# A kernel of attention, MLP and experts: an early unit's transposes moved by two iterations, row copies moved ahead of small steps, and a fold's first half in layer 1's bank

## The chip, the cores and the metric

One core of a Trainium2 chip runs the whole program. The metric is the device time of one execution in microseconds (us), as the median of several runs. Five engines work side by side, each through a queue of its own in order: TensorE (PE) does the matmuls, ScalarE (ACT) and VectorE (DVE) the elementwise work, GpSimd (POOL) small arithmetic and the indirect DMAs (gathers and scatters by a list of indices), SyncE (SP) issues the plain DMAs. They wait for each other only through semaphores.

## What is computed

Three stages, each feeding the next. (Cut from the reference.)

```python
# 1. attention with 32 memory slots per head; 4 batches, 8 heads, 576 tokens, head size 64
a = softmax(phi);  k_m = a^T k;  v_m = a^T v
attn_out = softmax(q k_m^T / 8) v_m
x = attn_out as (2304 tokens, 512)
# 2. MLP with an elu, 512 -> 2048 -> 512
h = x @ w_in
x = where(h > 0, h, exp(min(h, 0)) - 1) @ w_out
# 3. eight experts, the best two for every token
noisy = x @ w_gate + log1p(exp(x @ w_noise)) * noise
top2, top2_w = the two largest of noisy, and their softmax
for e in range(8):
    out[tokens of e] += top2_w * (relu(x[tokens of e] @ w1[e]) @ w2[e])
```

## The kernel before

Tokens lie in tiles of 128. The work of stages 2 and 3 is a flat list of 160 iterations `i`, each one slice of 128 hidden units of one *unit*. Units 0 to 3 are the MLP on blocks of 4, 5, 4 and 5 token tiles, 16 iterations each (i = 0 to 63). Units 4 to 7 are the *early* units: the first 256 tokens of experts 0 to 3, taken from blocks 0 and 1, 8 iterations each (i = 64 to 95). Units 8 to 11 take the rest of these experts (i = 96 to 127), units 12 to 15 the other four experts (i = 128 to 159).

An iteration does layer 1 of its slice (`layer1`, L976: matmuls into a bank of PSUM called `ph`, of which there are two, used in turn) and, two iterations behind (`LAG`), layer 2 (`layer2`, L1026 to L1028: three matmuls per token tile into the accumulators `acc0` to `acc4`). An MLP slice of 576 columns is cut in two, so it takes both `ph` banks; a bank comes free when DVE has done the last elu step on it (L991). Between the two, ACT and DVE apply elu or relu and split the result into a high and a low part. `prep_hi` and `prep_lo` (L568, L574) split the weights of coming iterations in the same way. When layer 2 of a unit's last slice is done, `put_rows` copies its accumulators to SBUF: L1036 (DVE) and L1034 (ACT) for the MLP, which then go to DRAM, L1047 (DVE) and L1045 (ACT) for an expert unit, which POOL then adds to the output (L1049).

The MLP's first weights are not multiplied with x but with the values of the attention, which is done ahead of time: `fold` (L488) makes the product on PE in two halves and `halve` (L137 on ACT, L138 on DVE) splits each. In units 1 and 3 all five accumulators are in use, so that one spare bank (`px`) is left (`single()` says so); there the fold is called from inside layer 2 (`between`), in front of its tile 3, at f = 2, 6, 10 and 14 of the unit where a fold is due: one half goes to `px`, the other to a bank of `ph`.

Around this, smaller jobs are written as generators: the attention of the next block, the routing of a finished block (`gating`), the fetching of an early unit's tokens (`fetch`: it reads the list of token numbers and gathers their rows, L880) and their transposes on PE (`spread`, L895, four 128x128 transposes of one tile). They stand in two queues, `heads` and `tails`. `tick` takes a step of them at three places of an iteration: at its start, in the middle (behind layer 1), and late (in front of layer 2); a generator says by what it yields which place it wants next. `drain` runs a generator to its end when its unit begins. Indirect DMAs that must not come in a heap are put on the list `spaced`; each call of `beat` sends one: a tiny copy on ACT (L616, four buffers), a tiny copy on POOL that waits for it (L617), and then the DMA on POOL, for instance a write to the expert lists (L799). A second table, `plan`, holds the steps of the other units' tokens by iteration (`route`: gathers L920, stores L925, loads L931).

Of the kernel before, what the change touches and what calls it, by code (L numbers as in the profile page):

```python
# [37 lines left out]
LAG = 2  # L38
# [4 lines left out]
def moe_stack_kernel(ctx, tc, phi, kv, kvt, q, wmlp, wgn, noise, wmoe, out):  # L43
# [22 lines left out]
    def bank(tag="px", bufs=1):  # L66
        return ps.tile([P, 512], F32, tag=tag, name=tag, bufs=bufs)
# [412 lines left out]
    def fold(b, j, gs):  # L480

        if (b, j) not in folds:
            folds[b, j] = [fp.tile([P, 2, 512], F32R, tag=n, name=n) for n in ("fh", "fl")]
        bks = {g: bank("ph", 2) if single() and g else side_bank() for g in gs}
        for p in range(4):
            for g in gs:
                o, m = slice(64 * g, 64 * g + 64), slice(32 * p, 32 * p + 32)
                pe.matmul(bks[g][m], att["vT", b][o, m], raws["a", 16 * b + 4 * j + p][o], start=True, stop=True,  # L488
                          tile_position=(64 * g, 32 * p))
        for g in gs:  # L490
            later(lambda g=g: halve(bks[g], *(t[:, g] for t in folds[b, j])))
# [127 lines left out]

    def drain(gen):  # L620
        place[0] = ""
        while spaced:
            beat()
        for queue in (heads, tails):
            while gen in queue:
                try:
                    next(queue[0])
                except StopIteration:
                    wants.pop(id(queue.pop(0)), None)
# [382 lines left out]
    def layer2(u, f, i, gh, gl, tiles=None, between=None):  # L1012
        if f == 0:
            u["acc"] = [bank("acc%d" % t) for t in range(u["nt"])]
        if i >= NRAW:
            wh, wl = ready["b", i]
        for t in range(u["nt"]) if tiles is None else tiles:
            if t == 3 and between:
                between()
            m = size(u, t)  # L1020
            o = slice(t * P, t * P + m)
            acc = u["acc"][t][:m]
            if i < NRAW:
                pe.matmul(acc, gh.bitcast(F32)[:, o], raws["b", i], start=f == 0, stop=f == u["nf"] - 1)
                continue
            pe.matmul(acc, gl[:, o], wh, start=f == 0, stop=False)  # L1026
            pe.matmul(acc, gh[:, o], wl, start=False, stop=False)  # L1027
            pe.matmul(acc, gh[:, o], wh, start=False, stop=f == u["nf"] - 1)  # L1028
# [83 lines left out]
    for i in range(len(flat)):  # L1112
# [3 lines left out]
        if i < len(flat):  # L1116
            u, f = flat[i]
            k = units.index(u)
            if f == 0:
                if "need" in u:  # L1120
                    drain(u["need"])
                if k == 1:
                    paced += zeros
                if k == 4:
                    moe["pair"] = True
                if k == 3:
                    side_stack.close()
                    moe["pool"] = ctx.enter_context(tc.tile_pool(name="moe", bufs=1))
                if k >= 3 and k + 1 < len(units):
                    n = units[k + 1]  # L1130
                    n["x"] = new_x()
                    if k == 3 or k + 1 == late:
                        n["need"] = spread(n)
                        (tails if k == 3 else heads).extend([fetch(n, [n]), n["need"]] if k == 3 else [n["need"]])
                    if k == 3:
                        for m, s in zip(units[5:late], [(-30, -26, -22, -18), (-42, -36, -28, -20), (-56, -42, -32, -22)]):
                            route(m, flat.index((m, 0)), s)
                        for m in units[late + 1:]:
                            route(m, flat.index((m, 0)))
            if k == late + 4 and f == 2:  # L1140
                tails.append(overflow_table())
            if k in (1, 2) and f == 0:
                paced = att_loads(k + 1) + paced
            if k < 3 and f == 0:
                n = units[k + 1]
                n["need"] = attention(k + 1)
                heads.append(n["need"])
            if k and u["kind"] == "mlp" and f == 0:
                u["x"] = att["x", k]
            j = (i + 2) // 4  # L1150
            turn_ = u["kind"] == "mlp" and f % 4 > 1 and j < 16

            within = turn_ and single() and f % 4 == 2 and i > 13 and j
            turn_ = turn_ and not single() and f % 4 == 3
            if i < 14:
                turn_ = f % 2 == 1
            elif turn_ or within:
                while ("vT", j // 4) not in att:
                    step_on(heads[0])
            if i >= 14 and turn_:  # L1160
                place[0] = ""
                fold(j // 4, j % 4, [0, 1])
            tick("", turn_ if i > 13 else i % 2 == 0)
            for step in plan.pop(2 * i, []):
                step()
            hidden_c()
            nxt = []
            if u["kind"] == "mlp":
                nxt += [("b", k) for k in ([14, 15] if i == 15 else [i] if i > 15 else [])]
            if 64 <= i + 2 < len(chunks):  # L1170
                nxt += [("a", i + 2), ("b", i + 2)]
            prep_hi(nxt)
            if u["kind"] == "moe" and i % 2 == 0:
                beat()
            gh = gp.tile([P, 640], F32R, tag="gh", name="gh")
            gl = gp.tile([P, 640], F32R, tag="gl", name="gl")
            cuts = splits(u)
            if u["kind"] == "mlp":
                elu, parts = ep.tile([P, 2, S], F32, tag="elu", name="elu"), []
            for j, (s0, n) in enumerate(cuts):  # L1180
                ph = layer1(u, i, s0, n)
                if j == len(cuts) - 1:
                    tick("mid", bool(within or turn_ and i < 14))
                o = slice(s0, s0 + n)
                if u["kind"] == "mlp":
                    elu_a(elu, ph, o)
                    parts.append((ph, o))
                else:
                    relu_(ph, gh, gl, o)
                if j == 0:  # L1190
                    beat()
            ahead = nxt[:1] if 61 < i < 64 else nxt
            prep_lo(ahead)
            settle()
            for n in at_end.get(i, []):
                load_to(n)
            for _ in range(0 if i == 0 else 2 if f < 10 else 1):
                if paced:
                    paced.pop(0)()
            if u["kind"] == "mlp":  # L1200
                if i < 2:
                    warm(4)
                if i == 0 or 1 < i < 14 and turn_:
                    fold_half((f + 1) // 2 or 1, split=True)
                elu_b(u, f, elu, parts, gh, gl)
                prep_lo(nxt[len(ahead):])
                settle()
                if i == 2:
                    warm(7)
                if i:  # L1210
                    conv2(pieces(i))
                keep(pieces(i))
                if i:
                    conv1_hi(pieces(i + 1))
                    conv1_lo(pieces(i + 1))
            tick("late")
            if u["kind"] == "mlp":
                beat()
            for step in plan.pop(2 * i + 1, []):
                step()  # L1220
            pend.append((u, f, i, gh, gl))
        else:
            tick()
        if i >= LAG and i < len(flat) - 1:
# [6 lines left out]
            if pf == pu["nf"] - 1:  # L1231
                for t in range(pu["nt"]):
                    put_rows(pu, t, pu["acc"][t])
                if pu["kind"] == "mlp":
                    b = pu["blk"]
                    if b < 3:
                        back = []
                        for t in range(pu["nt"]):
                            plan.setdefault(2 * (i + 2 + t // 2), []).append(lambda b=b, t=t, back=back: reload(b, t, back))
                    if b < 2:  # L1240
                        tails.append(gating(b, back))
                    elif b == 2:
                        heads.append(gating(b, back))
                    else:
                        heads.append(gating(b, pu["rows"]))
                    if b == 3:
                        heads.append(fetch(units[late], [units[late]], 4))


    for t in range(units[-1]["nt"]):  # L1250
# [74 lines left out]
```

## Time and profile before

| | before |
|---|---|
| median of 3 runs | 875.8 us (875.69 to 875.85) |
| the profiled execution, whole | 877.42 us |
| its span, first to last instruction | 875.7 us |
| PE busy | 843.8 us, 96% of the span |
| DVE, ACT, POOL busy | 567.3, 438.4, 202.6 us |
| mean clock granted to PE | 0.991 of full speed |

PE is the engine that is nearly always busy; the others have a third or more of the span free. The rows further down come from the same profiled execution. A row of a timeline reads: start in us, duration in us, engine, line and operation, output<-input, shape, xcount of merged instructions, and in brackets the idle time of the engine just before it and what ended it. The durations of matmuls overlap, since they are pipelined.

### The profile page before, as it was taken

The page shows a single profiled execution, that of the slowest core. Times are in us where ns is not written, and L with a number is a line of the kernel's source. Part 1 is how long each engine was busy: PE and PEld are TensorE (multiplying, and loading weights), DVE is VectorE, ACT ScalarE, POOL GpSimd, SP SyncE. Part 2 cuts the span into 40 slices and gives each one's busy share as a digit, 9 for nine tenths or more (in the row PEclk, how much of TensorE's full clock was granted, in tenths as well). Part 3 has the DMA queues.
Part 4 walks back from the last instruction along what each step waited for, and adds up shares of the span by engine and source line. Part 5 has one row for each costly group of instructions (what it writes and reads, how often), then busy time and mean ns, then how long its engine had stood idle before and what let it go on. Part 6 is the DMA issues. An engine that isn't in the chain of part 4 may idle for free. (4 is left out here: it accounts for less than half of the span.)

```text
span 875.7 us, 15408 instructions
## 1 busy us (share of the span) xinstructions
PE 843.8 (96%) x5688; PEld 698.4 (80%) x5691; DVE 567.3 (65%) x1200; ACT 438.4 (50%) x1007; POOL 202.6 (23%) x319
## 2 busy tenths in 40 slices
PE   8999999999998999979989999999999999999995
PEld 5566567777876778868778998888899999999994
DVE  5878887689768887766787765655657444454321
ACT  4767666555664555545646654544444333342311
POOL 1000100001323147124327421322412050120303
PEclk9999999999999999999999999999999999999998
DMA  9996678963852346453789987878996675452404
GB/s 349 345 385 224 220 272 285 329 222 141 295 172 86 97 148 142 110 180 121 206 229 216 286 247 240 235 236 244 287 247 186 181 166 170 142 122 97 59 1 60
DMA packets 100575, 174.65 MB, mean 199 GB/s; under 512 B 14610, under 2 KB 52370, under 8 KB 99474
## 3 DMA queue, kind: packets, MB, share of 16 engines
q1 hardware_dynamic: 90514, 152.93, 54.7%
q0 software_dynamic: 9984, 20.72, 12.0%
q8 instruction: 45, 0.74, 0.3%
q14 instruction: 32, 0.26, 0.1%
HBM read 132.01 MB, written 41.61 MB: 198 GB/s over the span
## 5 line engine op out<-in xcount | busy, mean ns | idle before, releaser
L1026 PE MATMUL acc<-bh,gl 128*128 128x512 f32 (+1 forms) x552 | 220.1, 399 | 1.5 <-DVE rows L1047 1.4
L1027 PE MATMUL acc<-bl,gh 128*128 128x512 f32 (+1 forms) x552 | 216.3, 392 | 0.0
L1028 PE MATMUL acc<-bh,gh 128*128 128x512 f32 (+1 forms) x552 | 216.0, 391 | 0.0
L1005 DVE SCALAR_TENSOR_TENSOR gl<-ph,gh 128x312 fp32r<-128x312 f32 (+2 forms) x128 | 61.6, 482 | 195.0 <-ACT gh L1004 194.9
L568 ACT ACTIVATE bh<-raw 128x512 fp32r<-128x512 f32 x144 | 90.0, 625 | 71.0 <-PE acc L1028 71.0
L1026 PEld LDWEIGHTS acc<-bh,gl 128*128 128x128 f32 (+1 forms) x552 | 103.0, 187 | 27.4 <-issue 7.5
L1028 PEld LDWEIGHTS acc<-bh,gh 128*128 128x128 f32 (+1 forms) x552 | 102.9, 186 | 23.6
L1004 ACT ACTIVATE gh<-ph 128x312 fp32r<-128x312 f32 (+2 forms) x128 | 55.0, 430 | 124.5 <-PE ph L976 124.5
L1027 PEld LDWEIGHTS acc<-bl,gh 128*128 128x128 f32 (+1 forms) x552 | 103.1, 187 | 17.3
L1049 POOL DMA_INDIRECT out<-rows,ids x40 | 65.0, 1624 | 203.6 <-DVE rows L1047 168.3
L574 DVE TENSOR_TENSOR bl<-raw,bh 128x512 fp32r<-128x512 f32 x144 | 99.0, 688 | 6.1 <-ACT bh L568 6.1
L976 PE MATMUL ph<-xl,ah 128*128 128x312 f32 (+2 forms) x512 | 94.4, 306 | 0.0
L976 PE MATMUL ph<-xh,al 128*128 128x312 f32 (+2 forms) x512 | 93.8, 305 | 0.0
L976 PE MATMUL ph<-xh,ah 128*128 128x312 f32 (+2 forms) x512 | 93.7, 305 | 0.0
L976 PEld LDWEIGHTS ph<-xl,ah 128*128 128x128 f32 x512 | 83.0, 188 | 8.2
L976 PEld LDWEIGHTS ph<-xh,al 128*128 128x128 f32 x512 | 79.1, 188 | 0.0
L976 PEld LDWEIGHTS ph<-xh,ah 128*128 128x128 f32 x512 | 78.8, 188 | 0.0
L976 PE MATMUL ph<-tl,fh 128*128 128x288 f32 x256 | 61.7, 323 | 5.9 <-DVE elu L991 3.2
L574 DVE TENSOR_TENSOR al<-raw,ah 128x512 fp32r<-128x512 f32 x96 | 65.5, 682 | 0.0
L920 POOL DMA_INDIRECT xg<-x2d,ids x35 | 37.2, 1064 | 120.8 <-DMA ids<-lst 70.1
L990 DVE SCALAR_TENSOR_TENSOR elu<-elu 128x288 f32<-128x288 f32 x128 | 58.4, 456 | 9.2 <-ACT elu L982 9.1
L981 ACT ACTIVATE elu<-ph 128x288 f32<-128x288 f32 x128 | 52.3, 408 | 22.4 <-PE ph L976 21.1
(265 smaller groups left out, 1230.4 us busy)
## 6 DMA issues: line engine op xcount, KB each, us to landing
raw<-in_wmoe SPq DMA_DIRECT2D x48, 1024.0 KB, 6.1
raw<-in_wmlp SPq DMA_DIRECT2D x32, 512.0 KB, 5.4
raw<-wxa SPq DMA_DIRECT2D x12, 1024.0 KB, 6.0
raw<-wxb SPq DMA_DIRECT2D x12, 1024.0 KB, 5.6
xs<-xg SPq DMA_DIRECT2D x35, 256.0 KB, 6.4
xq<-xs SPq DMA_DIRECT2D x140, 64.0 KB, 4.9
kv<-in_kv SPq DMA_DIRECT2D x8, 1024.0 KB, 13.1
out<-zrow SPq DMA_DIRECT2D x13, 512.0 KB, 9.4
```

Source lines behind the costliest of these rows:

```text
L568: act.activation(ready[h, c][0], raws[h, c], AF.Copy)
L574: dve.tensor_tensor(lo, raws.pop((h, c)), hi.bitcast(F32), op=OP.subtract)
L920: pool.indirect_dma_start(out=xg, out_offset=None, in_=x2d[:rows], in_offset=bass.IndirectOffsetOnAxis(ap=n["ids"][:, t, 0:1], axis=0))
L976: pe.matmul(ph, w, x, start=k == 0, stop=k == len(terms) - 1)
L981: act.activation(t[:, 0, o], ph, AF.Exp)
L990: dve.scalar_tensor_tensor(m, t[:, 0, o], 1.0, m, op0=OP.add, op1=OP.mult)
L1004: act.activation(gh[:, o], ph, AF.Relu)
L1005: dve.scalar_tensor_tensor(gl[:, o], ph, 0.0, gh[:, o].bitcast(F32), op0=OP.max, op1=OP.subtract)
L1026: pe.matmul(acc, gl[:, o], wh, start=f == 0, stop=False)
L1027: pe.matmul(acc, gh[:, o], wl, start=False, stop=False)
L1028: pe.matmul(acc, gh[:, o], wh, start=False, stop=f == u["nf"] - 1)
L1049: d = pool.indirect_dma_start(out=out, out_offset=bass.IndirectOffsetOnAxis(ap=ids[:m, t, 0:1], axis=0), in_=r, in_offset=None, compute_op ...
```

## The change

Five edits in four functions.

- `fold`: with one spare bank, the first half goes to layer 1's bank and the second to the spare one (before: the other way round). The halves are split in that order, so the one in `ph` comes first.
- `layer2`: where it is called for the first slice of a unit (f = 0), the fold inside it stands in front of tile 4 and no longer tile 3.
- `drain`: the list `spaced` is emptied only as long as the drained generator is still queued; before, it was emptied in any case.
- the first early unit (unit 4) gets a `fetch` that lets two more iterations pass between its gathers and its transposes.
- in an iteration in which layer 2 ends a unit, the late `tick` comes behind `layer2` and `put_rows`, no longer in front, and the late `beat` of an MLP iteration is left out.

```diff
-        bks = {g: bank("ph", 2) if single() and g else side_bank() for g in gs}
+        bks = {g: side_bank() if g or not single() else bank("ph", 2) for g in gs}
...
     def drain(gen):
         place[0] = ""
-        while spaced:
-            beat()
         for queue in (heads, tails):
             while gen in queue:
+                while spaced:
+                    beat()
                 try:
                     next(queue[0])
...
-            if t == 3 and between:
+            if t == 3 + (f == 0) and between:
                 between()
...
-                        (tails if k == 3 else heads).extend([fetch(n, [n]), n["need"]] if k == 3 else [n["need"]])
+                        (tails if k == 3 else heads).extend([fetch(n, [n], 2), n["need"]] if k == 3 else [n["need"]])
...
-            tick("late")
-            if u["kind"] == "mlp":
-                beat()
+            ends = i >= LAG and pend[0][1] == pend[0][0]["nf"] - 1
+            if not ends:
+                tick("late")
+                if u["kind"] == "mlp":
+                    beat()
             for step in plan.pop(2 * i + 1, []):
                 step()
             pend.append((u, f, i, gh, gl))
...
                     if b == 3:
                         heads.append(fetch(units[late], [units[late]], 4))
+                if i < len(flat):
+                    tick("late")
```

PE at the start of i = 60, near the end of unit 3, before: the last tile of layer 2 (`acc_4012`), the transposes of the early unit's first tile (`xg`, the gathered rows), layer 1, and the transposes of its second tile.

```order
L1028 MATMUL acc_4012<-bh,gh 128x512
L895 MATMUL px<-ident,xg 128x128 x4
L976 MATMUL ph<-tl,fh 128x288 x2
L976 MATMUL ph<-th,fl 128x288 x2
L976 MATMUL ph<-th,fh 128x288 x2
L976 MATMUL ph<-tl,fh 128x288 x2
L976 MATMUL ph<-th,fl 128x288 x2
L976 MATMUL ph<-th,fh 128x288 x2
L895 MATMUL px<-ident,xg 128x128 x4
```

The same engine after, at the start of i = 62, where the first tile's transposes stand now; the row behind layer 1 belongs to the gating of block 2.

```order
L1028 MATMUL acc_4012<-bh,gh 128x512
L895 MATMUL px<-ident,xg 128x128 x4
L976 MATMUL ph<-tl,fh 128x288 x2
L976 MATMUL ph<-th,fl 128x288 x2
L976 MATMUL ph<-th,fh 128x288 x2
L976 MATMUL ph<-tl,fh 128x288 x2
L976 MATMUL ph<-th,fl 128x288 x2
L976 MATMUL ph<-th,fh 128x288 x2
L752 LDWEIGHTS ones
```

Both transposes moved: the first from the start of i = 60 to that of i = 62, the second from the middle of i = 60 to the start of i = 63.

ACT at the start of unit 4 (i = 64), before: the last elu copies of unit 3, the beats, the weight splits and the relu (L1004).

```order
L997 ACTIVATE gh<-elu 128x576
L1000 ACTIVATE gh<-rest 128x64
L616 ACTIVATE beat<-top 1x1 x8
L568 ACTIVATE ah<-raw 128x512
L568 ACTIVATE bh<-raw 128x512
L1004 ACTIVATE gh<-ph 128x256
```

The same engine and place after.

```order
L997 ACTIVATE gh<-elu 128x576
L1000 ACTIVATE gh<-rest 128x64
L616 ACTIVATE beat<-top 1x1
L568 ACTIVATE ah<-raw 128x512
L568 ACTIVATE bh<-raw 128x512
L616 ACTIVATE beat<-top 1x1
L1004 ACTIVATE gh<-ph 128x256
L616 ACTIVATE beat<-top 1x1
```

The eight beats in a row are gone; they stand one by one between the other work of i = 63 to 68.

DVE in i = 73, where layer 2 ends unit 4, before: a weight split, steps of the gating of block 3 (`g_...`) and the row copy (L1047).

```order
L574 TENSOR_TENSOR bl<-raw,bh 128x512
L763 COPY g_cnt<-acc_5595 128x48
L768 TENSOR_SCALAR g_den<-g_e_5561 128x5
L769 RECIPROCAL g_rec<-g_den 128x5
L770 TENSOR_TENSOR g_rec<-g_rec,g_e_5561 128x5
L771 TENSOR_TENSOR g_pos<-g_cnt,ecap 128x40
L779 TENSOR_TENSOR g_pos<-g_pos,g_adj 128x5x4
L1047 TENSOR_SCALAR rows<-acc_5200,ids 128x512
```

The same engine and place after.

```order
L574 TENSOR_TENSOR bl<-raw,bh 128x512
L763 COPY g_cnt<-acc_5595 128x48
L1047 TENSOR_SCALAR rows<-acc_5192,ids 128x512
L768 TENSOR_SCALAR g_den<-g_e_5561 128x5
L769 RECIPROCAL g_rec<-g_den 128x5
L770 TENSOR_TENSOR g_rec<-g_rec,g_e_5561 128x5
L771 TENSOR_TENSOR g_pos<-g_cnt,ecap 128x40
L779 TENSOR_TENSOR g_pos<-g_pos,g_adj 128x5x4
```

The row copy moved in front of five small steps.

## Rows read from the trace of the kernel before

**Rows 1.** The waits of PE over the span: us in total, times, longest.

```profile
PE px L895 <- DMA xg<-x2d,ids: 4.5, 1, 4.5
PE ph L976 <- DVE elu L991: 3.2, 3, 1.8
PE px L661 <- DVE rows L1036: 1.9, 1, 1.9
PE ph L976 <- DVE fl L138: 1.7, 3, 0.8
...
PE acc L1026 <- DVE rows L1047: 1.4, 1, 1.4
```

**Rows 2.** PE's timeline from i = 59 to i = 62.

```profile
375.37 0.43 PE L976 MATMUL ph<-tl,fh 128*128 128x288 f32 x2
...
385.01 1.11 PE L895 MATMUL px<-ident,xg 128*128 128x128 f32 x4 [4.46 <-DMA xg<-x2d,ids]
...
388.58 0.60 PE L895 MATMUL px<-ident,xg 128*128 128x128 f32 x4
...
392.45 0.42 PE L976 MATMUL ph<-tl,fh 128*128 128x288 f32 x2
...
397.46 0.42 PE L976 MATMUL ph<-tl,fh 128*128 128x288 f32 x2
```

**Rows 3.** PE by microsecond: busy, (count), granted clock, DMA share, GB/s.

```profile
276.00:277.00 1.00, 1.00 (x35) 0.50 0.00 0
385.00:386.00 1.00, 0.99 (x5) 0.50 0.77 238
420.00:421.00 1.00, 1.00 (x11) 1.00 2.01 57
```

**Rows 4.** POOL's timeline, the first gather of unit 4.

```profile
378.12 1.02 POOL L880 DMA_INDIRECT xg<-x2d,ids  x1 [0.16 <-issue]
```

**Rows 5.** ACT's timeline at i = 64.

```profile
414.12 0.20 ACT L616 ACTIVATE beat<-top 1x1 f32<-1x1 f32 x1 [1.11 <-POOL tiny L617]
...
415.28 0.36 ACT L1004 ACTIVATE gh<-ph 128x256 fp32r<-128x256 f32 x1
```

**Rows 6.** The timelines of DVE and PE at the end of i = 65.

```profile
418.74 1.89 DVE L1036 COPY rows<-acc 128x512 f32<-128x512 f32 x3
...
419.48 0.66 PE L661 MATMUL px<-ident,rows 128*128 128x128 f32 x4 [1.93 <-DVE rows L1036]
```

**Rows 7.** The timelines of DVE and PE at i = 73 and 74.

```profile
449.85 0.16 DVE L768 TENSOR_SCALAR g_den<-g_e 128x5 f32<-128x5 f32 x1
...
450.67 0.74 DVE L1047 TENSOR_SCALAR rows<-acc,ids 128x512 f32<-128x512 f32 x1
...
451.47 0.50 PE L1026 MATMUL acc<-bh,gl 128*128 128x512 f32 x1 [1.41 <-DVE rows L1047]
```

**Rows 8.** The timelines of DVE and PE at the folds of i = 18 and 50.

```profile
140.56 0.69 DVE L138 TENSOR_TENSOR fl<-px,fh 128x512 fp32r<-128x512 f32 x1 [1.29 <-ACT fh L137]
141.16 0.68 DVE L138 TENSOR_TENSOR fl<-ph,fh 128x512 fp32r<-128x512 f32 x1
...
141.90 0.54 PE L976 MATMUL ph<-tl,fh 128*128 128x288 f32 x2 [0.83 <-DVE fl L138]
...
326.63 1.04 PE L488 MATMUL px<-raw,vT 64*32 64x512 f32 x2
327.62 0.61 PE L488 MATMUL ph<-raw,vT 64*32 64x512 f32 x1
```

**Rows 9.** The timelines of DVE and PE, i = 62 to 64.

```profile
399.40 0.26 DVE L763 COPY g_cnt<-px 128x32 f32<-128x32 f32 x2 [0.31 <-PE px L759]
...
406.34 0.46 DVE L991 SCALAR_TENSOR_TENSOR elu<-ph,elu 128x288 f32<-128x288 f32 x1
...
407.72 0.63 PE L976 MATMUL ph<-xl,ah 128*128 128x256 f32 x4
```

**Rows 10.** The waits of POOL over the span, one line.

```profile
POOL xg L920 <- DMA ids<-lst: 70.1, 4, 24.8
```

## The prediction

> **What bounds the kernel now.** I read the page first: TensorE (PE) is busy 843.8 of 875.7 us, so only time in which PE stands still, or runs at the lower of its two clocks, can be won. Next came PE's list of waits over the whole span [rows 1]. Its five longest lines are the ones to look at: 4.5 us in one wait of the first early unit's transposes (L895) for a gather, 3.2 us in three waits of layer 1 for DVE's last elu step, 1.9 us of one transpose of block 3's rows (L661) for the copy-out of those rows, 1.7 us in three waits of layer 1 for a fold's low half, and 1.4 us of layer 2 for an expert unit's row copy (L1047). The diff touches four of the five; no line of it stands near the elu waits (unit 2, before 275 us). Then I looked at each place in the timelines of PE, ACT, DVE and GpSimd (POOL), numbering iterations i = 0 to 159 as the kernel does. Behind the last of these places, at 451 us, PE has no further wait until its last matmul: whatever is won before that is kept, unless it uncovers a new wait.
>
> **Part 1: the early unit's transposes go from i = 60 to i = 62 and 63.** The first gather is issued at 378.12 [rows 4], PE starts on its tile at 385.01 after standing 4.46 us [rows 2]. From the start of layer 1 in i = 59 (375.37) to that of i = 61 (392.45) are 17.08 us; the undisturbed i = 61 takes 397.46 - 392.45 = 5.01, so two iterations should take 10.02 and the pair has 7.06 too much. In it are the two transposes themselves, which are only moved and not saved: 0.60 us each at full clock as the row has it, a little less where their ends overlap the next matmuls; I take 0.5 each. That leaves 7.06 - 1.0 = 6.1 us (5.8 if they cost their full 0.60). Of it 4.5 is the gap and 1.6 what PE loses behind it: the row of the microsecond behind the gap shows a granted clock of 0.50, which is 1.2 of 2.4 GHz [rows 3]. Will the wait come back two iterations later? The first transposes then stand 10 us behind the place where PE now begins to wait, and the gather lands 4.5 us behind that place, so 5.5 us are to spare; the second tile's transposes at 388.58 had no wait even now, and they move by three starts of an iteration. The gathers stay where they are in POOL's order, and so do the DMAs in SP's.
>
> A gap doesn't always cost clock: behind the 1.9 us at L661 the granted clock is 1.00, behind the longest elu wait (1.8 us) it is 0.50 [rows 1, 3]. The Trainium skill, "TensorE: Matmul & The Clock Gate", section "Part 1: The HAM clock gate (the "warmup" mystery)", says that the point at which the clock changes depends on a phase that isn't tied to the kernel and differs from run to run; by that rule the timed runs need not have had this fall, and the change would bring 1.6 us less. The trace agrees in so far as two gaps of nearly one length end differently. It is rival B below.
>
> **Part 2: the drain at unit 4's start.** Before, i = 64 pushes eight beats through ACT at once. Each is a small ACT copy that a POOL copy must answer, and there are four buffers, so from the fifth on ACT waits for POOL: the last beat begins at 414.12 after waiting 1.11 [rows 5]. Layer 1 of i = 64 began on PE at 407.72 [rows 9], but its relu comes on ACT only at 415.28 [rows 5]. DVE follows, so that the first row copy of block 3 begins at 418.74 and PE stands 1.93 us in front of L661 [rows 6]. After, the generator to be drained is no longer queued, so the loop pushes nothing, and the beats go out one or two per iteration from i = 63 to 68. A beat is 0.20 us of ACT [rows 5]; POOL answers each together with its list write, and one or two of these fit beside an iteration. The relu then follows its matmuls, and the row copy the first finished accumulator, whose last matmul stands four tiles of layer 2 in front of L661. DVE has the relu's low part, two weight splits and the copy to do in that time, which is about as long. I take 2.0 (the gap and its refill); bounds 1.0, if DVE is late for half of it, and 2.1.
>
> **Part 3: rows ahead of the small steps.** At i = 73 DVE does five small steps between 449.85 and the start of the row copy at 450.67; PE waits 1.41 us for that copy [rows 7]. The copy now stands in front of these five: 450.67 - 449.85 = 0.82 us earlier, and PE with it. The small steps behind it end where they ended, as the sum of DVE's work is the same. So 0.8; bounds 0.3, if the copy finds its accumulator or DVE late, and 1.4, the whole wait. At the ends of units 0 to 3 the same swap moves one exp on ACT (i = 49), about 0.1, and no wait of PE hangs on it: nothing.
>
> **Part 4: the folds.** In units 1 and 3 a fold is split over the spare bank px and a bank of layer 1's pair (ph). Layer 1 of the next iteration needs the ph bank back, but its half is turned second: ACT px, ph, DVE px, ph. With the ph half first, that bank is free one DVE step earlier, 141.16 - 140.56 = 0.60 us [rows 8]. At i = 19 PE waits 0.83 us there [rows 8], at i = 31 about 0.7 of the 1.7 in rows 1, both more than 0.60, so each gives 0.60. At i = 50 the wait lies in two places: the fold's first ph matmul at 327.62 follows the first px matmul (326.63) by 1 us, since ph isn't free yet [rows 8], and i = 51 has the small rest of the 1.7; with the fold behind tile 3 the first shrinks, and the second is set by ACT and DVE again, 0.60 earlier. The other four folds have no wait worth counting. Sum 1.8, with 0.1 for i = 27: 1.9. Below: 1.0, if ACT, which at i = 18 has an exp of the attention to do in front of the fold's first half, holds it back. Above: 2.6, all that rows 1 and the hidden 1 us hold. The spare bank is now free 0.60 later. Its next user is a transpose or a gating product at least one layer 1 behind, so nothing.
>
> **Sum.** 6.1 + 2.0 + 0.8 + 1.9 = 10.8 us. It is made against the profiled execution (span 875.7, in all 877.4); the median of the runs is 875.8, and I take the same 10.8 off it: **865.0 us**. With all lower bounds (part 1 without its clock term: 4.2) it is 6.5 off, 869.3; with all upper ones (6.3 + 2.1 + 1.4 + 2.6) 12.4, 863.4.
>
> **Rivals.** *A, a new wait from DVE's load.* The two splits of the early unit (a DVE subtraction of 0.69 us each, the size of the fold's low half [rows 8]) now lie in i = 62 and 63, which also hold the gating's steps. DVE there frees the ph bank that i = 64 needs when its first elu step ends, 406.34 + 0.46 = 406.80, and PE takes it at 407.72 [rows 9]: 0.9 us of slack. For it: 2 x 0.69 us plus about 1 us that DVE waits for the transposes and ACT's half, 2.4 in all. Against it: that slack, the 1.0 by which the two transposes delay PE, and 0.31 us that DVE is idle in i = 62 [rows 9], 2.2 in all. So it comes out nearly even; if DVE is later than that, PE loses 1 to 3 us: 866 to 868. *B, the clock isn't won back:* as one of two gaps of nearly one length costs clock and the other none, the timed runs of before may lack the fall behind the 4.46 us; then 1.6 less is won, 866.6. *C, the gap only moves*, as the gather lands later or the transposes wait elsewhere: part 1 falls to about 1, 870. Against it stands the 5.5 us of room. *D, slower.* With the beats spread, POOL does list writes between the gathers of the early units, and a beat behind a held gather holds ACT from the fifth on, as the eight did. POOL's waits for a list of indices reach 24.8 us [rows 10]. If one such hold fell between i = 64 and 68, ACT would stand for it less four beats (some 8 us), 16.8 us, and the whole would end at 875.8 - 10.8 + 16.8 = 882; from a hold of 19 us on the change loses. Against it: the lists for those gathers are read before i = 61, so the long waits lie elsewhere. *E, nothing happens:* the built order shows all four moves, so hardly.
>
> **How the numbers follow.** Forecast (863.4 to 866): 0.62; A 0.16; B 0.09; C 0.06; D 0.04; E and others 0.03. Range 862.9 to 869.0: it takes the forecast, A, B and nearly all lower bounds, and leaves out C, D and E, 0.13, with a little on the low side. 0.2% is 1.75 us, about what a measurement of this kernel can tell from no change: faster 0.94, same 0.02, slower 0.04.
>
> **What would show it.** Right: no wait of L895 in PE's list and full clock through i = 60 to 64; beats on ACT one by one with the relu of i = 64 within a microsecond of its matmuls; no wait at L661; the wait for L1047 down to about 0.6; waits for fl down to about 0.3 and 0.1; the elu waits and the one for g_oh (i = 73) as they were. Wrong: a wait of layer 1 at i = 64 for DVE (A), a wait of L895 at i = 62 (C), ACT standing in front of a beat (D). If a later chain, such as unit 8's gathers, turns out to have been waiting on time that these gaps gave it, the new wait would stand at its transposes near i = 90.

## The result

The changed kernel takes 864.4 us (median of 4 runs, 863.3 to 865.0), the kernel before 875.8 us on the same chip (874.3 to 875.9): a ratio of 0.9873 with a 95% interval of 0.9856 to 0.9890, or 11.4 us less. The forecast was 865.0 us, 10.8 us less. In two later sets of runs, on chips 8 and 2, the unaltered pair gave 0.9886 (0.9863 to 0.9909) and 0.9875 (0.9859 to 0.9891); the chip of the first pair is not on record.

The profiled execution after took 864.7 us, its span 862.9 us; TensorE (PE) is busy 838.0 us, 97% of the span, at a mean clock of 0.997. PE's list of waits after (us in total, times, longest) answers to [rows 1]:

```profile
PE ph L976 <- DVE elu L991: 3.2, 3, 1.8
PE acc L640 <- DVE x2T L650: 1.9, 2, 1.0
...
PE acc L754 <- DVE g_oh L743: 1.3, 1, 1.3
PE ph L976 <- DVE fl L138: 1.1, 2, 0.9
PE ph L488 <- DVE elu L991: 1.1, 3, 0.7
...
PE acc L1026 <- DVE rows L1047: 0.5, 1, 0.5
```

The waits for L895 (4.5 us) and at L661 (1.9) are gone, the one for L1047 fell from 1.4 to 0.5. The waits for elu stand as they were. The wait for fl only fell from 1.7 to 1.1, and the fold's first matmul (L488) now waits for an elu step. The 1.9 us for x2T are no loss of the change: an unaltered kernel before (`before_again`, below) has them too.

To see where the time went I took, in either trace, the time from the start of layer 1 (L976) in each iteration to that of the next, and subtracted. Two pairs are shown: the runs of the prediction and its result, and a second pair of unaltered kernels, both on chip 2 (experiments `before_again` and `after_third`). Iterations that are not named differ by no more than 0.09 us, apart from the last one, whose stretch runs to the end of the span (0.4 us shorter in the first pair).

| iterations | forecast | first pair | second pair |
|---|---|---|---|
| 59 to 63 (part 1) | -6.1 | -6.15 | -6.87 |
| 65 (part 2) | -2.0 | -2.15 | -1.72 |
| 73, 74 (part 3) | -0.8 | -0.76 | -0.75 |
| 18, 19, 27, 30, 31, 50, 51 (part 4) | -1.9 | -0.86 | -2.07 |
| 41 to 43 (not touched) | 0 | -0.02 | +0.01 |
| ahead of i = 18 (not touched) | 0 | -2.44 | +0.31 |
| sum | -10.8 | -12.4 | -11.1 |

The first pair's traces differ by 12.8 us, of which 2.4 lie in the first 30 us, where nothing was changed: 1.0 ahead of the first layer 1, and 1.4 where PE ran at the lower clock (1.2 of 2.4 GHz) in before, from 26.5 to 29.9 us, and not in after. The second pair differs by 0.3 us there. The parts alone sum to 9.9 us in the first pair and 11.4 in the second.

Three of the four places, after. The first gather is issued by GpSimd (POOL) at 374.77, and the transposes that need its rows stand on PE at 387.07 and 392.78, without a wait and at full clock (compare [rows 2, 4]; a timeline row is start, duration, engine, line and operation, and in brackets the idle time ahead):

```profile
374.77 1.02 POOL L880 DMA_INDIRECT xg<-x2d,ids  x1 [0.16 <-issue]
...
387.07 0.60 PE L895 MATMUL px<-ident,xg 128*128 128x128 f32 x4
...
392.78 0.60 PE L895 MATMUL px<-ident,xg 128*128 128x128 f32 x4
```

At i = 64 and 65 the beats stand one by one on ACT, the relu (L1004) of i = 64 begins at 400.78, 2.6 us behind the start of its layer 1 (398.23) instead of 7.6, and DVE's row copies begin at 406.70, while PE is still in layer 2, so L661 has no wait (compare [rows 5, 6]):

```profile
400.69 0.18 ACT L616 ACTIVATE beat<-top 1x1 f32<-1x1 f32 x1
400.78 0.36 ACT L1004 ACTIVATE gh<-ph 128x256 fp32r<-128x256 f32 x1
...
406.70 2.09 DVE L1036 COPY rows<-acc 128x512 f32<-128x512 f32 x3
...
398.23 0.63 PE L976 MATMUL ph<-xl,ah 128*128 128x256 f32 x4
...
407.90 0.60 PE L661 MATMUL px<-ident,rows 128*128 128x128 f32 x4
```

At i = 73 the row copy stands in front of the small steps, and PE waits 0.53 us for it, not 1.41 [rows 7]:

```profile
438.26 0.74 DVE L1047 TENSOR_SCALAR rows<-acc,ids 128x512 f32<-128x512 f32 x1
438.92 0.16 DVE L768 TENSOR_SCALAR g_den<-g_e 128x5 f32<-128x5 f32 x1
...
439.06 0.50 PE L1026 MATMUL acc<-bh,gl 128*128 128x512 f32 x1 [0.53 <-DVE rows L1047]
```

### The profile page after: what moved, and what is told of

The parts are those of the page before. It is cut to its first block, busy times and chain, and to the rows that moved or that the text cites. A ratio compares the mean times of both kernels' runs of the same rounds, so it can differ in the third digit from the quotient of the medians.

```text
span 862.9 us, 15413 instructions
## 1 busy us (share of the span) xinstructions
PE 838.0 (97%) x5688; PEld 694.4 (80%) x5691; DVE 567.1 (66%) x1200; ACT 437.8 (51%) x1007; POOL 202.3 (23%) x319
## 5 line engine op out<-in xcount | busy, mean ns | idle before, releaser
L1004 ACT ACTIVATE gh<-ph 128x312 fp32r<-128x312 f32 (+2 forms) x128 | 55.0, 430 | 125.1 <-PE ph L976 125.1
L976 PE MATMUL ph<-xl,ah 128*128 128x312 f32 (+2 forms) x512 | 94.4, 306 | 0.0
L976 PE MATMUL ph<-xh,al 128*128 128x312 f32 (+2 forms) x512 | 93.8, 305 | 0.0
L976 PE MATMUL ph<-xh,ah 128*128 128x312 f32 (+2 forms) x512 | 93.6, 305 | 0.0
L976 PEld LDWEIGHTS ph<-xl,ah 128*128 128x128 f32 x512 | 83.0, 188 | 8.2
L976 PEld LDWEIGHTS ph<-xh,al 128*128 128x128 f32 x512 | 79.1, 188 | 0.0
L976 PEld LDWEIGHTS ph<-xh,ah 128*128 128x128 f32 x512 | 78.8, 188 | 0.0
L976 PE MATMUL ph<-tl,fh 128*128 128x288 f32 x256 | 60.9, 319 | 5.4 <-DVE elu L991 3.2
L997 ACT ACTIVATE gh<-elu 128x576 fp32r<-128x576 f32 (+1 forms) x50 | 33.0, 660 | 59.3 <-DVE elu L991 59.3
```

What stands on the lines that cost most here:

```text
L976: pe.matmul(ph, w, x, start=k == 0, stop=k == len(terms) - 1)
L997: act.activation(gh[:, o], m, AF.Copy)
L1004: act.activation(gh[:, o], ph, AF.Relu)
```

## The experiments

### Each part alone

Theory: the four parts act at four places and add up. Rival: a part only moves its wait on, and the sum needs all of them. Four kernels, each the kernel before with one part, on one chip (5), where the kernel before took 878.6 us.

`p1_transposes`: the two iterations more between gathers and transposes.

```diff
-  extend([fetch(n, [n]), n["need"]] ...)
+  extend([fetch(n, [n], 2), n["need"]] ...)
```

> The kernel before with part 1 alone (transposes of the first early unit two iterations later). Theory (the gap and the clock behind it go, the transposes are only moved): 6.1 us less, some 869.6; no wait of L895, the 1.9 us at L661 and the 1.4 at L1047 stay. Rival A (DVE's load in i = 62 and 63): a wait of layer 1 at i = 64 of 1 to 3 us, some 871 to 873. Rival B (no fall of the clock behind the gap in timed runs): 4.5 less, 871.3.

`p2_drain`: the drain empties the list only while its generator is queued.

```diff
-        while spaced:
-            beat()
         for queue in (heads, tails):
             while gen in queue:
+                while spaced:
+                    beat()
```

> The kernel before with part 2 alone (the drain empties the spaced list only while its generator is queued). Theory: the relu of i = 64 is no longer behind eight beats, the wait at L661 (1.9 us) goes, 2.0 less, some 873.7; the 4.5 us wait of L895 stays. Rival: DVE's weight splits and not the beats make the row copy late, then at least 1 us of the wait stays and the gain is under 1.

`p3_rows`: the late `tick` behind `layer2` and `put_rows` where a unit ends, and no late `beat` there.

```diff
-            tick("late")
-            if u["kind"] == "mlp":
-                beat()
+            ends = i >= LAG and pend[0][1] == pend[0][0]["nf"] - 1
+            if not ends:
+                tick("late")
+                if u["kind"] == "mlp":
+                    beat()
...
+                if i < len(flat):
+                    tick("late")
```

> The kernel before with part 3 alone (rows copied out ahead of the late steps). Theory: the wait for L1047 falls from 1.4 to 0.6, 0.8 less, some 874.9, all else as before. Rival: the copy finds its accumulator late, the wait stays, no change.

`p4_folds`: the two edits of the folds.

```diff
-  bks = {g: bank("ph", 2) if single() and g else side_bank() for g in gs}
+  bks = {g: side_bank() if g or not single() else bank("ph", 2) for g in gs}
...
-  if t == 3 and between:
+  if t == 3 + (f == 0) and between:
```

> The kernel before with part 4 alone (fold's first half in layer 1's bank, behind tile 3 at f = 0). Theory: 0.6 each at i = 19, 31 and 50 to 51 and 0.3 at i = 27, 2.0 less, some 873.7. Rival from the trace of the changed kernel: at i = 18 DVE waits for the DMA of phi, whose landing is tied to absolute time, so what is won before it (and the 0.6 there) is lost again: 1.2 to 1.5 less. In the trace the two are told apart by a wait of DVE for phi near 131 to 134 us.

| kernel | ratio to before (95%) | us by the ratio | us at its place in the trace |
|---|---|---|---|
| p1_transposes | 0.9934 (0.9916 to 0.9952) | -5.8 | -5.8 (i = 59 to 63) |
| p2_drain | 0.9984 (0.9974 to 0.9993) | -1.4 | -2.15 (i = 65) |
| p3_rows | 0.9992 (0.9980 to 1.0004) | -0.7 | -0.79 (i = 73, 74) |
| p4_folds | 0.9981 (0.9972 to 0.9991) | -1.7 | -2.1 (i = 18 to 51) |

The places were compared with the profiled execution of the kernel before, of the first set of runs. Elsewhere these traces differ from it too: i = 58 is 0.3 to 0.8 us longer in all four, whichever part they carry. The ratios add up to 9.6 us, which with these intervals doesn't contradict the 11.4 of the whole change. p3_rows alone can't be told from no change by its time, but its trace has the gain at its place. In p1_transposes the waits of the other three parts stand as before, and only L895 is gone:

```profile
PE px L661 <- issue: 2.5, 1, 2.5
PE ph L976 <- DVE fl L138: 1.7, 3, 0.8
...
PE acc L1026 <- DVE rows L1047: 1.4, 1, 1.4
```

("issue" means that the profile shows nothing that PE waited for; the row copy of before stood there.) So the parts act where the prediction put them, and apart from each other. The times alone don't separate p1_transposes from the 4.5 us of rival B (its interval is 4.2 to 7.4 us less); its trace does, by 5.8 us at the place. In p2_drain something is given back: i = 67 and 68 took 0.94 and 1.09 us more, i = 73 0.7 more. The changed kernel of the first pair, which has the same part, gives nothing back there (i = 67 and 68 in 4.73 and 3.48 us, as before), and the next two groups show where it does.

### The distance to the transposes, and the drain

On another chip (8; before 877.8 us) the changed kernel was run with distances of one and three iterations, and with part 2 undone.

`after_again`: the changed kernel, unaltered.

> The changed kernel once more, unaltered, as the scale for the other three kernels of this call. The theory that its gain is the four parts (6.1 + 2.1 + 0.8 + 0.9 to 2.0, and nothing that hangs on one chip) expects a ratio to the kernel before of 0.985 to 0.989 here too. On the chip of the first four experiments PE stood 2 to 4 us at i = 66 in the kernels that keep the old drain, with no engine named for the wait; the rival, that the kernel before is disturbed there on some chips and the changed one is not, expects a larger gain where before is slower, a ratio of 0.980 to 0.985.

`x_one` and `x_three`:

```diff
-  fetch(n, [n], 2)
+  fetch(n, [n], 1)     # x_one
+  fetch(n, [n], 3)     # x_three
```

> The changed kernel with the early unit's transposes one iteration later than before, where the change has two. My theory of part 1: the first tile's gather lands when it lands, 4.5 us behind the place where the kernel before wanted it, and one iteration is 5.0 us, so the transposes at i = 61 find the rows there with some 0.5 us to spare: a wait of L895 of 0 to 0.5 us, no clock lost, the time within 0.5 us of the changed kernel on the same chip. The rival: what counts is how the gathers stand to the other DMAs of i = 60 to 62, so that they land later when the transposes do not wait for them, and a wait of 1 to 3 us comes back at i = 61, perhaps with the clock: 1 to 4 us slower than the changed kernel.

> The changed kernel with the transposes three iterations later than before. The second tile's transposes and its split are then still queued when unit 4 begins and are run by the drain, with all beats of the list in a heap once more. My theory: the heap costs its 2.0 us (the wait of L661 at the end of i = 65 is back, 1.5 to 2 us), and layer 1 of i = 64 waits for the split that now stands directly in front of it, ACT's half and DVE's 0.69 us and their start, some 2 us: 3.5 to 5 us slower than the changed kernel. The rival, that room of any size in front of the transposes is good and the drain has little to do with it: within 1 us of the changed kernel.

`u2_drain_back`: the old drain in the changed kernel (the diff of `p2_drain`, reversed).

> The changed kernel with part 2 alone undone: the drain at the start of unit 4 empties the list in any case. My theory: the eight beats stand in a row on ACT at i = 64, the relu comes some 7 us behind its matmuls, DVE's row copies are late and the wait of L661 at the end of i = 65 is back with 1.8 to 2.0 us: 2.0 us slower than the changed kernel. The rival: part 2 gives less than that, because beats spread over i = 63 to 68 hold ACT and POOL there, as the run of part 2 alone showed (1.0 and 1.1 us more at i = 67 and 68): 0 to 1 us slower.

| kernel | median (lowest to highest), us | ratio to before (95%) |
|---|---|---|
| after_again | 868.9 (866.5 to 869.3) | 0.9886 (0.9863 to 0.9909) |
| x_one | 868.7 (868.0 to 868.8) | 0.9894 (0.9875 to 0.9912) |
| x_three | 870.6 (868.7 to 873.8) | 0.9913 (0.9879 to 0.9948) |
| u2_drain_back | 869.8 (869.4 to 871.7) | 0.9913 (0.9891 to 0.9935) |

*after_again* gave 0.9886, inside its theory's 0.985 to 0.989; the larger gain that the rival expected where before is slower (0.980 to 0.985) didn't come.

*x_one* settles part 1: one iteration of room is enough. The first transposes begin at 382.46 with no wait, 7.3 us behind the issue of their gather; the waits of 3.7 to 4.5 us in the six kernels that turn the tile at i = 60 ended between 6.3 (`before_again`) and 6.9 us (before) behind theirs. The rival, that the rows come later when nobody waits for them, fell; in the three traces of kernels with part 1 that show this landing (after, `after_third`, `phi_counts_late`) it lies 6.5 to 6.9 us behind the issue as well.

```profile
375.17 1.02 POOL L880 DMA_INDIRECT xg<-x2d,ids  x1 [0.16 <-issue]
...
382.46 0.60 PE L895 MATMUL px<-ident,xg 128*128 128x128 f32 x4
```

*u2_drain_back* brings the heap back, the eight beats in a row on ACT (the last one below) and a wait of PE at L661, as the theory said:

```profile
404.72 0.20 ACT L616 ACTIVATE beat<-top 1x1 f32<-1x1 f32 x1 [1.11 <-POOL tiny L617]
```

```profile
PE px L661 <- DVE bl L574: 2.5, 1, 2.5
...
PE acc L640 <- ACT x2T L663: 1.6, 1, 1.6
```

Against `after_again` i = 65 and 66 are 2.73 and 1.69 us longer, but i = 67, 68, 73 and 74 are 2.6 shorter and i = 90 0.3. The timed difference is 0.9 us by the medians, inside the rival's 0 to 1, and 2.4 by the two ratios, near the theory's 2.0; their intervals overlap, so that the times don't decide. The theory's wait is in the trace, and so is time given back, as the rival said.

*x_three* has the heap too (wait at L661 2.6 us), by the span of its trace 2.8 us more, by the medians 1.7 with a wide spread, so that the time alone doesn't tell it from `after_again`. The second term that I expected, a wait of layer 1 at i = 64 for the split, is not there: layer 1 begins at 400.49 without a wait, since both tiles' transposes came into i = 63 (394.28 and 396.34). What a distance of three brings back is the heap, and no second wait.

Part of what moves between i = 65 and 74 are waits with no engine named, and part are waits for ACT's copy of x2T (L663). At i = 73 it is the wait for g_oh, 1.9 us in `p2_drain`, `after_again` and `x_one` and 1.1 to 1.3 in the other traces that have it. On this chip and that of the first group, `after_again`, `x_one` and `p2_drain` take 5.5 to 5.7 us for i = 67 (else 4.7) and 3.9 to 4.6 for i = 68 (else 3.5); the five kernels with a heap (p1, p3, p4, x_three, u2) take 6.1 to 8.7 for i = 66 (else 4.7), in p1, p3 and x_three with a part of it at the lower clock. In `after_again` PE stands in the middle of 32 small matmuls of the gating, of which 24 have run on the same operand, while the DMA queues move 400 GB/s (columns: us, busy, count, granted clock, DMA share, GB/s):

```profile
415.71 0.38 PE L640 MATMUL acc<-wgs,x2T 128*32 128x16 f32 x24
416.41 0.30 PE L640 MATMUL acc<-wgs,x2T 128*32 128x16 f32 x8 [0.32 <-issue]
```

```profile
415.00:416.00 1.00, 0.86 (x29) 1.00 1.03 404
416.00:417.00 1.00, 0.68 (x23) 1.00 1.10 403
```

### Part 4 taken apart, the kernel before once more, and the next step

On chip 2, before 876.1 us.

`before_again` and `after_third`: unaltered.

> The kernel before, unaltered. On two chips every kernel that keeps the old drain spent 2.0 to 4.0 us more in i = 66 than the kernel before did in the run that the prediction rests on, in waits with no engine named, and the kernel before was 1 to 3 us slower there. Theory: this is a wait of the old drain's heap that the first run was spared by chance, so the kernel before shows it too, with i = 66 at 6.5 to 9 us for 4.7. Rival: it belongs to the edits that were tried, and i = 66 takes 4.7 us here.

> The changed kernel, unaltered, as the scale on this chip for the other kernel that is timed here. Theory: a ratio to the kernel before of 0.985 to 0.989. In its trace the theory of the phi load (see the other kernel) expects DVE to wait for phi at i = 18 only if PE came through i = 0 without its slow first microseconds (i = 0 in 3.5 us, not 4.8): then i = 18 and 19 take 7.0 and 6.5 us, else 6.2 and 6.1.

`p4_banks`: the kernel before with the first of the two edits of `p4_folds` alone.

> The kernel before with only the first half of part 4: the fold's first half in layer 1's bank, and the fold of i = 50 still in front of tile 3. It tells the two edits of part 4 apart. Theory: i = 18, 19, 27 and 31 gain what they gained with both (0.3, 0.3, 0.3 and 0.6 us), and i = 50 gains 0.3 to 0.4 of its 0.7, since the first ph matmul now stands in front and waits 0.3 us longer for the bank there. Rival: at i = 50 the whole comes from the order of the banks, 0.7, and the place of the fold is worth nothing.

`phi_counts_late`: the changed kernel with phi loaded earlier and the routing's counts behind the row copies.

```diff
+            if k in (0, 1) and f == 10:
+                load_phi(k + 2)
             if k in (1, 2) and f == 0:
-                paced = att_loads(k + 1) + paced
+                paced = att_loads(k + 1)[1:] + paced
...
-        yield "next" if blk < 2 else "pe"
+        yield "next" if blk < 2 else "late" if blk == 3 else "pe"
```

> The changed kernel with two more moves. The phi block of the next attention is loaded six iterations earlier (at i = 10 and 26, not 16 and 32), and the six small matmuls that count block 3's routing (with the wait for g_oh) stand behind layer 2 and the row copies of i = 73, no longer in front. Theory: what part 4 lost in the profiled run of the changed kernel, 1.2 us at i = 18 and 19, was the wait of DVE for phi, so these take 6.2 and 6.1 us here however early PE is; and PE's wait for g_oh (1.3 to 1.9 us, with the clock behind it in one run) goes, as layer 2 needs nothing of it: i = 73 and 74 together 1.0 to 1.5 us shorter. In all 1.0 to 2.5 us faster than the changed kernel on the same chip. Rival: the wait of i = 73 only moves to layer 1 of i = 74 or to the counts behind layer 2, and the phi wait costs nothing in most runs: within 0.5 us of the changed kernel.

Measured: before_again 875.3 us in its one run, p4_banks 874.1 in its one run; after_third 864.45 (864.2 to 867.2), ratio 0.9875 (0.9859 to 0.9891); phi_counts_late 864.2 (863.7 to 865.9), ratio 0.9871 (0.9856 to 0.9886).

*before_again*: i = 66 takes 4.74 us here, so my theory that the stand at i = 66 belongs to the heap fell, and so did the rival that it belongs to the edits, as `after_again` has it at i = 67 and `after_third`, the same program, has not. It shows in every kernel traced on chips 5 and 8, and in the first pair and on chip 2 in none, but for 0.7 us at i = 68 and 69 of `p4_banks`; it lies at i = 66 with a heap and at i = 67 and 68 without. What PE waits for there stays open, and with one trace of each kernel it isn't shown that the chip makes the difference. It fits that part 2 measures 1.4 us by time on chip 5 and 0.9 by the medians on chip 8, and 1.7 to 2.15 in the two pairs of traces.

*p4_banks*: with the banks' order alone, i = 18 gains nothing and i = 19 0.60, i = 27 and 31 0.32 and 0.61; i = 50 gains nothing and i = 51 0.41. The reason stands in one row: the fold's first ph matmul, now in front, waits 0.90 us for the elu step that frees the bank. Behind tile 4 (`after_third`) this wait is 0.22.

```profile
323.78 0.61 PE L488 MATMUL ph<-raw,vT 64*32 64x512 f32 x1 [0.90 <-DVE elu L991]
```

```profile
324.29 0.61 PE L488 MATMUL ph<-raw,vT 64*32 64x512 f32 x1 [0.22 <-DVE elu L991]
```

At i = 50 and 51 both edits give 0.62 together (`after_third`), the banks alone 0.41; at i = 18 and 19 both give 0.58 and the banks 0.60. So the second edit is worth 0.2 us, all of it at the fold of i = 50. The theory's sizes came, 0.3 to 0.4 for the banks at the fold of i = 50 and 0.6 for the fold of i = 18, but each one iteration later than it said; the rival's 0.7 didn't.

*phi_counts_late*: the wait for g_oh is gone, i = 73 is 1.49 us shorter, and i = 74 1.37 longer. The row copy now has the wait:

```profile
435.71 0.42 DVE L1005 SCALAR_TENSOR_TENSOR gl<-ph,gh 128x256 fp32r<-128x256 f32 x1 [1.35 <-ACT gh L1004]
...
437.25 0.75 DVE L1047 TENSOR_SCALAR rows<-acc,ids 128x512 f32<-128x512 f32 x1
...
438.05 0.51 PE L1026 MATMUL acc<-bh,gl 128*128 128x512 f32 x1 [1.82 <-DVE rows L1047]
```

1.82 us are what the two waits were together before the move, 1.30 for g_oh and 0.53 for the copy. Both hang on DVE, which does the relu's low part behind a wait for ACT, two weight splits and the copy whatever PE has to wait with; the rival was right that the wait only moves and the time stays, though it moved to the row copy and not to where the rival looked for it. The phi load, 32 us earlier (issued at 87.27), changed nothing here, since `after_third` has no wait for phi either. The two kernels are alike within what can be measured.

## Why the prediction was right, and where its steps were off

**Part 1 (6.1 forecast, 6.15 and 6.87 measured).** The gap went, and with it the lower clock. Rival B, that the clock isn't won back, rested on two gaps of one length with and without a fall. That holds for the elu gap and not for this one. All six kernels with the gap at L895 (3.7 to 4.5 us) show the granted clock at 0.50 behind it; in before_again it stays there from 382 to 388 us:

```profile
382.00:383.00 1.00, 0.72 (x4) 0.50 0.87 229
...
388.00:389.00 1.00, 1.00 (x5) 0.87 0.07 9
```

So i = 60 takes 1.27 us more there than in before, while i = 59, with a gap of 3.9 us and not 4.5, takes 0.55 less: that is the 0.7 us by which the second pair is larger. The gap's share was well sized; the clock's share (1.6) varies from run to run, upwards here, and with it part 1 passed its upper bound of 6.3, for which the prediction shows no working. The timed runs have no trace, but a mean clock: the 41 of the kernel before on chips 2, 5 and 8 have 0.990 to 0.995, below the 0.997 of the two traces without any fall (after, `phi_counts_late`). So none of them was without a fall, though where it lay they don't show. Rival C's condition is met by no run.

**Part 2 (2.0 forecast, 2.15 and 1.72).** The chain was as told: beats, relu, splits, row copy, L661. The first pair is a little above the bound of 2.1, and the second has less because the wait at L661 was 1.5 us there, not 1.9. Rival D would have shown as ACT standing in front of a beat; the beats after stand without brackets. Rival A would have shown as a wait of layer 1 at i = 64; the row at 398.23 above has none.

**Part 3 (0.8 forecast, 0.76 and 0.75).** The wait that is left, 0.53 us, is what I named (0.6).

**Part 4 (1.9 forecast, 0.86 and 2.07).** The size was right in the second pair and in p4_folds; in the first trace of the changed kernel one step failed. At i = 18 DVE waited for the load of phi in front of its maximum, which comes ahead of the elu step that frees the fold's bank, and PE waited twice behind it:

```profile
133.11 0.75 DVE L150 TENSOR_REDUCE nmx<-phi 128x1 f32<-128x576 f32 x1 [1.10 <-DMA phi<-in_phi]
...
136.37 0.61 PE L488 MATMUL ph<-raw,vT 64*32 64x512 f32 x1 [0.70 <-DVE elu L991]
...
140.06 0.53 PE L976 MATMUL ph<-tl,fh 128*128 128x288 f32 x2 [0.91 <-DVE fl L138]
```

That costs 1.2 us against after_third (i = 18 and 19 take 7.01 and 6.56 us in after, 6.24 and 6.13 in after_third). I first took it for the price of PE being 2.4 us early, as a load comes when it comes. The expectation of after_third said so, and it fell: after_third comes as fast through i = 0 and doesn't wait, and four more kernels with the same load (p1, p4_folds, p4_banks, before_again) reach i = 18 within 0.3 us of after and don't wait either. In p4_folds the load was issued at 120.51 and DVE read phi at 131.99; in after it was issued at 120.25 and landed at 133.1. So this load took at least 1.4 us longer in one run; why is not known. The three traces that show its landing have 10.6 us (p4_banks), 12.1 (before) and 12.8 (after); in before it landed only 0.6 us ahead of its use. So the spread of this load between runs (2.2 us) is larger than the slack that it had, and the prediction, which looked at ACT's exp at i = 18 and not at this load, had no term for it. Without it the wait for fl is 0.49 at i = 18 and 0.25 at i = 50 (after_third; I had named 0.3 and 0.1), and a new one of the folds' first matmul for elu, 0.4 in two places (i = 30 and 50), is what I hadn't foreseen. The term also had its parts shifted: I gave i = 27 0.1 and it gave 0.3, and I gave i = 19 alone 0.60, which came as 0.26 at i = 18 and 0.32 at i = 19 (second pair).

**What was not in the sum.** The first pair's start-up, 2.4 us, is no gain of the change: `after_again` has the lower clock at 26 us again. And the clock falls that are not tied to L895 don't cost what they seem to. At i = 41 PE waits 1.80 us for elu in before and after. In before the clock falls behind it [rows 3], in after it doesn't:

```profile
271.57 0.53 PE L976 MATMUL ph<-tl,fh 128*128 128x288 f32 x2 [1.80 <-DVE elu L991]
...
279.36 0.45 PE L640 MATMUL acc<-wgs,x2T 128*32 128x16 f32 x32 [0.94 <-DVE x2T L650]
...
272.00:273.00 1.00, 1.00 (x9) 1.00 0.00 0
```

After gains 1.48 us at i = 41 and gives 1.46 back in the next two iterations, in waits for DVE. The same trade stands between `phi_counts_late`, which has no fall here either, and `after_third`, which has it:

```profile
272.00:273.00 1.00, 1.00 (x6) 0.50 0.00 0
```

The Trainium skill, "TensorE: Matmul & The Clock Gate", section "Part 1: The HAM clock gate (the "warmup" mystery)", says that the point of the change depends on a phase that differs from run to run; the traces agree in so far as this gap of 1.7 to 1.8 us has either outcome (4 of 14 traces have the fall), while no run shows that a phase is the cause. What the fall costs is another matter: nothing where DVE is the bound, and 1.7 to 3.0 us at i = 59 and 60, where PE is (the six traces with the gap, i = 59 to 63 less those of after and less the gap).

So the timed gain, 11.4 us, agrees with the four parts as the second pair has them (11.4, by the table), and there the forecast's 10.8 fell short by the clock behind L895 (0.7), with part 2 0.3 below its term. The first pair's parts give 9.9. The forecast lies between the two, and that it met the time within 0.6 us is in part luck: the start-up (2.4 us), the clock behind L895 (1.3) and the phi load (1.2) each moved a trace by more.

One reading of the prediction was off without harm: it calls the lines of [rows 1] PE's five longest waits, but a wait of L432 for DVE, 1.7 us at the very start, is longer than the 1.4 us of L1047.

## What to carry to other kernels

A transpose that waits for a gather can be moved by what the trace shows as landing time; one iteration (5 us) was enough here for a wait of 3.7 to 4.5 us, and two cost nothing, while three ran into the next drain. Before moving work, ask whether the engine that the wait names has slack behind it: the row copy in front of five small steps did, the counts behind the row copy did not, as DVE was late for both. And of a lower clock, ask first which engine is the bound in that stretch, since where it isn't PE the lost time comes out of the next wait.

## What the runs showed of the hardware

- The start-up differs between runs of one kernel: i = 0 takes 3.45 us in nine traces and 4.8 in five, and the latter five all have the clock at 0.50 for some 3 us from 25.5 to 26.9 us on.
- The wait for g_oh of 1.9 us in `after_again` and `x_one` is followed by a clock of 0.50, from 439.5 and 438.5 us on, that of 1.9 us in `p2_drain` is not.
- In the traces of chips 5 and 8 PE loses 1 to 4 us at i = 66 to 68, and with the same program (`after_third`, after) nothing. DMA traffic doesn't tell them apart: the DMA queues move 400 GB/s at the stand in `after_again` and `x_one`, but also 404 GB/s at 413 us in after, which has no stand, and one in `p3_rows` begins at 422.58 us, where they move 49 GB/s.
- The 16 KB blocks on the queue of kind "instruction" that are loaded near i = 67 come 0.3 to 0.4 us behind the stand in `after_again` and `p2_drain`, and one is loaded at 415.9 in after, which has no stand; so they don't tell the traces apart either.
